# Attention and ELU feed-forward on one core: the feed-forward products and the turning of z and kv in two 128x64 column tiles

## The chip, the core and the metric

The kernel runs on one core of one Trainium2 chip. A core has a matrix engine (TensorE, PE in the profile, its weight loads listed apart as PEld), a vector engine (VectorE, DVE), a scalar engine (ScalarE, ACT), a general engine (GpSimd, POOL) and a queue engine that issues transfers (SyncE, SP). The engines run side by side and wait for each other through semaphores. The metric is the time of the kernel on the device in microseconds (us), as the median over several executions.

## What is computed

Two blocks follow each other, all in fp32. The attention block has no softmax. It makes features of queries and keys, sums over the sequence once for the whole batch, and divides:

```python
# q, k, v: (4, 4, 1088, 32); S1, S2: (8, 32)
def phi(x):                      # 64 features
    a, b = S1 x, S2 x            # 8 numbers each
    return outer(a, b)
kv  = sum over s of phi(k)[s] v[s]^T     # per batch and head, 64 x 32
z   = sum over s of phi(k)[s]            # per batch and head, 64
out = (phi(q) . kv) / (phi(q) . z + 1e-6)
```

The heads are put side by side, which gives x with 4352 tokens of 128 numbers. The second block is a feed-forward layer with 2048 hidden units:

```python
h = x @ w_in                             # 4352 x 2048
g = where(h > 0, h, exp(min(h, 0)) - 1)
return g @ w_out                         # 4352 x 128
```

The reference computes in double precision; the weights and the sketches S1, S2 arrive as 64-bit numbers and are rounded to fp32 on the core.

## The kernel before

**Tiling.** The 4352 tokens are cut into groups of 512 (the name is `g`): groups 0 to 7 have 512 tokens, group 8 has 256. The hidden units are cut into eight parts of 256 (`cp`), each of two chunks of 128 (`c`). One step of the main loop is one pair (g, cp): two products of w_in (`mm1`, into PSUM tiles `h`, one for each chunk), ELU on them (`elu`: two ScalarE instructions at L723 and L725, one VectorE instruction at L731 that writes `gg`), and two steps later the product with w_out that takes `gg` (`mm2`). The list `steps` holds the order: groups 0 and 1 alternate over cp, then groups 2 to 8 run one after the other.

**Order.** The order is written out by hand; no scheduler changes it. On each engine the instructions run in the order of the program. In step n the loop issues `mm1` of step n, then what is listed for that step under `at`, then the first ELU, what is listed under `mid`, the second ELU, what is listed under `late`, and last the w_out product of step n - 2. The attention of the later groups is listed in that way: `KF_late` (features of keys, tile `kfps`, small column and row tiles), `KA` (sums for kv and z, 32-column tiles, tile `kv`), `turn` (below), and `queries` (32x32 tiles at L493 and L589).

**Three forms of products.** A product on PE has a stationary operand, which is loaded first, and a moving one that streams through. The array can be used whole (128 rows by 128 columns) or in tiles, where a product names its tile by `tile_position`.

- Groups 0, 1 and 8 use the whole array: in `mm1` (L702), in `mm2` (L744, groups 0 and 1) and in `mm2_last` (L767, group 8). `mm1_first` (L714) is the first product of w_in.
- Groups 2 to 7 (`seven(g)`) use two tiles of 128 rows by 64 columns: `mm1` at L706 writes partitions 0 to 63 from the first 64 columns of w_in and partitions 64 to 127 from the other 64, with the same moving operand. Their second product is `mm2_seven` (L664), which computes four 64x64 blocks from seven products of sums (tiles `pa` and `pb`; the sums `tt` are made on GpSimd).
- The attention parts use smaller tiles.

**Turning.** For each batch, `Z` (L377) multiplies the sums z with a matrix of the sketch on the whole array, and `KV` (L391) turns two 128x128 blocks of kv with `nc.tensor.transpose`, also on the whole array. Batch 0 has its `Z` in `Z_first`, ahead of the main loop, followed by a filler product `keep_warm` (L218), and its `KV` in `KV_first`, step 8. Batches 1, 2 and 3 are turned by `turn` in steps 12, 20 and 28.

**Before the main loop**, the weights are rounded on VectorE and ScalarE (`RA`, `RB`, `RC`; L99 to L125), and the first tokens go through attention. PE then starts on w_out with the first L744.

The old forms are these:

```python
nc.tensor.matmul(hs[g, cp][c][:, :n], W[:, cp, c * P:c * P + P], xg[g][:, :n])            # L702
nc.tensor.matmul(hs[g, cp][c][r, :n], W[:, cp, c * P + 64 * u:c * P + 64 * u + 64],       # L706
                 xg[g][:, :n], skip_group_check=True, tile_position=(0, 64 * u))          # u = 0, 1
```

Of the kernel before, what the change touches and what calls it, by code (L numbers as in the profile page):

```python
# [27 lines left out]
def kernel(  # L28
# [21 lines left out]
    nc = tc.nc  # L50
    B, H, S, D = q.shape
    R = S1.shape[0]
    P = 128
# [92 lines left out]
    W = const.tile([P, NP, 4 * P], F32, name="W")  # L146
# [50 lines left out]
    ident = const.tile([P, P], F32, name="ident")  # L197
# [15 lines left out]

    idle = psum.tile([P, 512], F32, name="idle", tag="o0", bufs=1)

    def keep_warm(n, cols=256):
        for i in range(n):
            nc.tensor.matmul(idle[:, :cols], some[:, :P], some[:, :cols], skip_group_check=True)  # L218
# [16 lines left out]
    SXh = const.tile([P, FD], F32, name="SXh")  # L235
# [11 lines left out]
    SW = const.tile([FD, H, 3, R], F32, name="SW")  # L247
    SWq = const.tile([FD, B, 4, R], F32, name="SWq")
    keep_warm(3)
    keep_warm(1, 96)  # L250
    sps = psum.tile([P, 512], F32, name="sps", tag="aux")
    nc.tensor.matmul(sps[:, :2 * R], Sx[:].rearrange("p h d -> p (h d)"), ident[:2 * R, :2 * R])
    make_SXh()
    keep_warm(1)
    nc.vector.tensor_mul(Sab[:], _ap(sps[:, :2 * R], [[0, H], [1, 2 * R]]), _ap(bmask[:], [[1, H], [0, 2 * R]]))
    nc.gpsimd.tensor_copy(SW[:, :, :2, :].rearrange("p h x r -> p h (x r)"), Sab[:])
# [23 lines left out]
    kv_ps, kvz, feats, wzs, kf_ps = {}, {}, {}, {}, []  # L280
# [93 lines left out]

    def Z(b, ps, zl):

        nc.tensor.matmul(ps[:, 96:128], SXh[:], zl[:])  # L377

    def Z_out(b, ps):
        z = wzs[b] = SW[:, :, 2, :] if b == 0 else work.tile([FD, H, R], F32, name="wz", tag="wz")[:]  # L380
# [7 lines left out]

    def KV(b, ps):
        for f in range(2):  # L390
            nc.tensor.transpose(ps[:, 128 + P * f:128 + P * f + P], kvz[b][:, f].rearrange("p c s -> p (c s)"), ident[:])  # L391

    def KV_out(b, ps):
        nc.vector.tensor_copy(kvq[:, b].rearrange("p f h d -> p (f h d)"), ps[:, 128:384])
# [2 lines left out]
    def Z_first():  # L397
        ps = psum.tile([P, 512], F32, name="zps", tag="h", bufs=4)
        for i in range(KT):
            z_tile(0, ps, i)  # L400
        zl = ZC(0, ps)
        Z(0, ps, zl)
        Z_out(0, ps)
        keep_warm(1, 160)
# [7 lines left out]
    def KV_first():  # L412
        ps = psum.tile([P, 512], F32, name="kvps", tag="aux")
        KV(0, ps)
        KV_out(0, ps)
# [5 lines left out]
    abw, ans, qp, qpT, xg, xps = {}, {}, {}, {}, {}, {}  # L421
# [196 lines left out]
    hs, es, gs, ops = {}, {}, {}, {}  # L618
# [5 lines left out]
    def seven(g):  # L624
        return 2 <= g < NQ - 1
# [70 lines left out]
    def mm1(g, cp, cs=(0, 1)):  # L696
        n = qn[g] * P
        if 0 in cs and (g, cp) not in hs:
            hs[g, cp] = [psum.tile([P, 512], F32, name="h", tag="h", bufs=4) for c in range(2)]
        for c in cs:  # L700
            if not seven(g):
                nc.tensor.matmul(hs[g, cp][c][:, :n], W[:, cp, c * P:c * P + P], xg[g][:, :n])  # L702
                continue
            for u in range(2):
                r = slice(64 * u, 64 * u + 64)
                nc.tensor.matmul(hs[g, cp][c][r, :n], W[:, cp, c * P + 64 * u:c * P + 64 * u + 64], xg[g][:, :n],  # L706
                                 skip_group_check=True, tile_position=(0, 64 * u))

    def mm1_first():
        hs[0, 0] = [psum.tile([P, 512], F32, name="h", tag="h", bufs=4) for c in range(2)]  # L710
        for w in range(2):
            for c in range(2):
                cols = [x[:].rearrange("p (m w s) -> p w m s", w=2, s=P)[:, w] for x in (hs[0, 0][c], xg[0])]
                nc.tensor.matmul(cols[0], W[:, 0, c * P:c * P + P], cols[1], skip_group_check=True)  # L714

    def elu_a(g, cp, c, parts=(0, 1)):

# [20 lines left out]
    def mm2(g, cp, first, last):  # L738
        n = qn[g] * P
        if first:  # L740
            ops[g] = psum.tile([P, 512], F32, name="o", tag=f"o{g % 2}", bufs=1)
        gg = gs.pop((g, cp))
        for c in range(2):
            nc.tensor.matmul(ops[g][:, :n], W[:, cp, (2 + c) * P:(3 + c) * P], gg[:, c, :n],  # L744
                             start=(first and c == 0), stop=(last and c == 1))

    def fin1(g):
        n = qn[g] * P
# [11 lines left out]
    def mm2_last(cp, first, last):  # L760
        g = NQ - 1
        if first:
            ops[g] = [psum.tile([P, P], F32, name="ol", tag=t, bufs=k) for t, k in (("o0", 1), ("aux", 2))]
        gg = gs.pop((g, cp))
        for a in range(4):
            c, i = (a % 2, a // 2) if last else divmod(a, 2)
            nc.tensor.matmul(ops[g][i][:], gg[:, c, i * P:i * P + P], W[:, cp, (2 + c) * P:(3 + c) * P],  # L767
                             start=(first and c == 0), stop=(last and c == 1))

    def fin_last():  # L770
        g, n = NQ - 1, qn[NQ - 1]
# [31 lines left out]
    q5_early(0)  # L803
    q1_second()
    mm1_first()
    RA(2)
    RB(2)
    RC(1)
    elu_a(0, 0, 0)
    elu_a(0, 0, 1)  # L810
    mm1(0, 1)
    q2(1, 2)
    q4_early(1)
# [4 lines left out]
    elu_d(0, 0, 1)  # L818
    q5_early(1)
    mm2(0, 0, True, False)  # L820
    RC(3)
    for c in range(2):
# [40 lines left out]
    def turn(b):  # L863
        Z(b, kv_ps[b], zls.pop(b))
        KV(b, kv_ps[b])
# [53 lines left out]
    for n in range(2, N + 2):  # L919
        if n < N:  # L920
            g, cp = steps[n]
            mm1(g, cp)
        for f, *a in extra.get(n, ()):
            f(*a)
        if n < N:
            elu(g, cp, 0)
            if seven(g):
                sums7(g, cp, 0)
            for f, *a in extra.get((n, 0), ()):
                f(*a)  # L930
            elu(g, cp, 1)
            if seven(g):
                sums7(g, cp, 1)
        for f, *a in extra.get((n, 1), ()):
            f(*a)
        g, cp = steps[n - 2]
        if g == NQ - 1:
            mm2_last(cp, cp == 0, cp == NP - 1)
        elif seven(g):
            mm2_seven(g, cp, cp == 0, cp == NP - 1)  # L940
            if cp == NP - 1:
                fin_seven(g)
        elif n > 2:
            mm2(g, cp, cp == 0, cp == NP - 1)
            if cp == NP - 1:
                fin1(g)
# [30 lines left out]
```

## Time and profile before

| what | value |
|---|---|
| median of 5 runs | 274.61 us |
| the five runs | 272.47, 272.70, 274.61, 274.76, 275.01 us |
| profiled execution | 275.01 us, its span 273.2 us |
| granted PE clock, mean | 1.000 |
| MATMUL records: L706 / L702 / L744 / L767 | 384 / 92 / 64 / 64 |
| mean of one record: L706 / L702 / L744 | 593 / 522 / 604 ns |
| mean of one weight load: 64 columns / 128 columns | 137 / 190 ns |
| VectorE L731 (`gg`), 144 times | 652 ns each |
| ScalarE L723 and L725, 144 times each | 566 and 607 ns |
| GpSimd sums L644, L647, L648, L649, 48 times each | 754, 796, 770, 784 ns |

The profile is of one execution, the longest of the five. The records of PE overlap: a matmul's record runs from its start to the end of its results, so two that follow each other share a part, and the distance from start to start says what one costs. The weight loads run beside the products when nothing stands between. A group in the timeline ("x4") is a run of records of the same line; "128*64" is the size of the array tile in rows and columns, "128x512" the partitions and elements of the moving operand.

### The profile page before, as it was taken

The page shows a single profiled execution, that of the slowest core. Times are in us where ns is not written, and L with a number is a line of the kernel's source. Part 1 is how long each engine was busy: PE and PEld are TensorE (multiplying, and loading weights), DVE is VectorE, ACT ScalarE, POOL GpSimd, SP SyncE. Part 2 cuts the span into 40 slices and gives each one's busy share as a digit, 9 for nine tenths or more (in the row PEclk, how much of TensorE's full clock was granted, in tenths as well). Part 3 has the DMA queues.
Part 4 walks back from the last instruction along what each step waited for, and adds up shares of the span by engine and source line. Part 5 has one row for each costly group of instructions (what it writes and reads, how often), then busy time and mean ns, then how long its engine had stood idle before and what let it go on. Part 6 is the DMA issues. An engine that isn't in the chain of part 4 may idle for free.

```text
span 273.2 us, 7609 instructions
## 1 busy us (share of the span) xinstructions
PE 266.9 (98%) x3083; PEld 168.2 (62%) x3083; DVE 190.8 (70%) x350; ACT 183.5 (67%) x351; POOL 166.1 (61%) x233
## 2 busy tenths in 40 slices
PE   8999999999999999999999999999999999999994
PEld 5864444454442666666676666666766666667894
DVE  6599999996959796999548767464447444774552
ACT  2269978686564655676567667777677667777682
POOL 4500007303407986699969999988588988897200
PEclk9999999999999999999999999999999999999999
DMA  6995981001002300001100110001000200110021
GB/s 189 323 340 172 238 226 32 0 13 74 0 2 34 47 4 2 2 0 18 28 2 2 19 23 2 0 12 25 10 1 13 31 0 4 15 19 10 2 29 29
DMA packets 26419, 13.60 MB, mean 50 GB/s; under 512 B 19217, under 2 KB 24593, under 8 KB 26385
## 3 DMA queue, kind: packets, MB, share of 16 engines
q1 hardware_dynamic: 25792, 12.66, 18.8%
q8 instruction: 24, 0.39, 0.6%
q10 hardware_dynamic: 592, 0.46, 0.5%
q14 instruction: 11, 0.08, 0.1%
HBM read 10.88 MB, written 2.23 MB: 48 GB/s over the span
## 4 chain that ended last, share of the span: by engine, by line
PE 94%; DVE 4%; issue 1%; ACT 0%; DVEq 0%
PE h L706 30%; PE pb L664 16%; PE pa L664 12%; PE h L702 12%; PE o L744 11%; PE ol L767 3%; PE h L589 2%; PE idle L218 2%; PE kv L359 1%; PE abp L290 1%; PE qps L589 1%; DVE qp L536 1%; PE kfps L309 1%; PE h L493 1%; PE qps L493 1%
## 5 line engine op out<-in xcount | busy, mean ns | idle before, releaser
L731 DVE SCALAR_TENSOR_TENSOR gg<-e,h 128x512 f32<-128x512 f32 (+1 forms) x144 | 91.9, 652 | 64.7 <-ACT e L725 60.8
L723 ACT ACTIVATE e<-h 128x512 f32<-128x512 f32 (+1 forms) x144 | 81.6, 566 | 57.8 <-PE h L706 45.3
L706 PE MATMUL h<-xg,W 128*64 128x512 f32 x384 | 91.4, 593 | 0.0
L725 ACT ACTIVATE e<-e 128x512 f32<-128x512 f32 (+1 forms) x144 | 87.4, 607 | 4.6
L644 POOL TENSOR_TENSOR tt<-gg 128x256 f32<-128x256 f32 x48 | 36.2, 754 | 17.2 <-DVE gg L731 16.7
L706 PEld LDWEIGHTS h<-xg,W 128*64 128x64 f32 x384 | 27.9, 137 | 28.2 <-issue 24.9
L647 POOL TENSOR_TENSOR tt<-gg 128x256 f32<-128x256 f32 x48 | 38.2, 796 | 11.3 <-DVE gg L731 11.1
L649 POOL TENSOR_TENSOR tt<-gg,tt 128x256 f32<-128x256 f32 x48 | 37.6, 784 | 3.8
L648 POOL TENSOR_TENSOR tt<-tt,gg 128x256 f32<-128x256 f32 x48 | 37.0, 770 | 3.8
L664 PEld LDWEIGHTS pa<-gg,W 128*64 128x64 f32 x384 | 24.6, 137 | 22.4 <-issue 22.2
L702 PE MATMUL h<-xg,W 128*128 128x512 f32 (+1 forms) x92 | 36.6, 522 | 0.0
L744 PE MATMUL o<-gg,W 128*128 128x512 f32 x64 | 30.8, 604 | 0.4 <-DVE W L125 0.4
L664 PE MATMUL pa<-gg,W 128*64 128x128 f32 x384 | 30.3, 275 | 0.0
L664 PE MATMUL pb<-tt,SS 128*64 128x128 f32 x384 | 29.8, 273 | 0.0
L702 PEld LDWEIGHTS h<-xg,W 128*128 128x128 f32 x92 | 16.8, 190 | 14.9 <-issue 9.7
L664 PEld LDWEIGHTS pb<-tt,SS 128*64 128x64 f32 x384 | 23.4, 137 | 0.0
L744 PEld LDWEIGHTS o<-gg,W 128*128 128x128 f32 x64 | 11.4, 189 | 14.1 <-issue 11.9
L664 PE MATMUL pb<-gg,SS 128*64 128x128 f32 x192 | 19.5, 274 | 0.1
L664 PE MATMUL pb<-tt,W 128*64 128x128 f32 x192 | 19.4, 273 | 0.0
L122 POOL TENSOR_TENSOR raw<-raw,tiny 128x512 f32<-128x512 f32 x1 | 1.0, 1046 | 30.0 <-DVE raw L117 30.0
L664 PE MATMUL pa<-tt,SS 128*64 128x128 f32 x192 | 19.3, 273 | 0.0
L664 PEld LDWEIGHTS pb<-gg,SS 128*64 128x64 f32 x192 | 12.6, 137 | 1.0 <-issue 0.7
(141 smaller groups left out, 295.5 us busy)
## 6 DMA issues: line engine op xcount, KB each, us to landing
raw<-in_moe_w_in_dram SPq DMA_DIRECT2D x8, 256.0 KB, 5.8
raw<-in_moe_w_out_dram SPq DMA_DIRECT2D x8, 256.0 KB, 5.9
hd_k<-in_k_dram SPq DMA_DIRECT2D x3, 544.0 KB, 8.3
hd_q<-in_q_dram SPq DMA_DIRECT2D x3, 544.0 KB, 3.6
v<-in_v_dram SPq DMA_DIRECT2D x4, 288.0 KB, 6.8
out_dram<-ob SPq DMA_DIRECT2D x72, 16.0 KB, 1.5
v<-in_v_dram SPq DMA_DIRECT2D x4, 256.0 KB, 8.4
out_dram<-ob SPq DMA_DIRECT2D x16, 32.0 KB, 1.7
```

Of the source, the lines that this page charges most:

```text
L589: nc.tensor.matmul(ps[c][D * h:D * h + D, 64 * k:64 * (k + m)], kvq[r, b, f, h, :], qpT[g, i][r, n * o + 2 * k:n * o + 2 * (k + m), f, :], ...
L644: nc.gpsimd.tensor_tensor(t[:, 0], b12, b11, op=SUB)
L647: nc.gpsimd.tensor_tensor(t[:, 2], b22, b12, op=SUB)
L648: nc.gpsimd.tensor_tensor(t[:, 1], t[:, 2], b11, op=ADD)
L649: nc.gpsimd.tensor_tensor(t[:, 3], b21, t[:, 1], op=SUB)
L664: nc.tensor.matmul(bank[64 * u:64 * u + 64, P * col:P * col + P], lhs, rhs[:, u], start=(first and i in (0, 3)), stop=last, skip_group_che ...
L702: nc.tensor.matmul(hs[g, cp][c][:, :n], W[:, cp, c * P:c * P + P], xg[g][:, :n])
L706: nc.tensor.matmul(hs[g, cp][c][r, :n], W[:, cp, c * P + 64 * u:c * P + 64 * u + 64], xg[g][:, :n], skip_group_check=True, tile_position=( ...
L723: nc.scalar.activation(e, hs[g, cp][c][:, :n], RELU, scale=-1.0)
L725: nc.scalar.activation(e, e, EXP, scale=-1.0)
L731: nc.vector.scalar_tensor_tensor(gs[g, cp][:, c, :n], es[g, cp][:, c, :n], -1.0, hs[g, cp][c][:, :n], op0=ADD, op1=MAX)
L744: nc.tensor.matmul(ops[g][:, :n], W[:, cp, (2 + c) * P:(3 + c) * P], gg[:, c, :n], start=(first and c == 0), stop=(last and c == 1))
```

## The change

A helper `halves` issues one product as two, in the two 128x64 column tiles. It takes the place of every whole-array product from the first one of w_in on: `mm1_first`, `mm1` (where it also takes the place of the loop that groups 2 to 7 had), `mm2` and `mm2_last`; and of `Z` for all four batches and of the transposes in `KV`, which become products with the identity as moving operand. The filler products, the transposes of query features in `q4_early` and the transpose in `KS_first` stay on the whole array. Nothing else is changed, and the order of the program is the same.

```diff
+    def halves(dst, lhs, rhs, **kw):
+        for u in range(2):
+            nc.tensor.matmul(dst[64 * u:64 * u + 64], lhs[:, 64 * u:64 * u + 64], rhs, skip_group_check=True,
+                             tile_position=(0, 64 * u), **kw)
...
     def Z(b, ps, zl):
 
-        nc.tensor.matmul(ps[:, 96:128], SXh[:], zl[:])
+        halves(ps[:, 96:128], SXh[:], zl[:])
...
     def KV(b, ps):
         for f in range(2):
-            nc.tensor.transpose(ps[:, 128 + P * f:128 + P * f + P], kvz[b][:, f].rearrange("p c s -> p (c s)"), ident[:])
+            halves(ps[:, 128 + P * f:128 + P * f + P], kvz[b][:, f].rearrange("p c s -> p (c s)"), ident[:])
...
         for c in cs:
-            if not seven(g):
-                nc.tensor.matmul(hs[g, cp][c][:, :n], W[:, cp, c * P:c * P + P], xg[g][:, :n])
-                continue
-            for u in range(2):
-                r = slice(64 * u, 64 * u + 64)
-                nc.tensor.matmul(hs[g, cp][c][r, :n], W[:, cp, c * P + 64 * u:c * P + 64 * u + 64], xg[g][:, :n],
-                                 skip_group_check=True, tile_position=(0, 64 * u))
+            halves(hs[g, cp][c][:, :n], W[:, cp, c * P:c * P + P], xg[g][:, :n])
...
-                nc.tensor.matmul(cols[0], W[:, 0, c * P:c * P + P], cols[1], skip_group_check=True)
+                halves(cols[0], W[:, 0, c * P:c * P + P], cols[1])
...
         for c in range(2):
-            nc.tensor.matmul(ops[g][:, :n], W[:, cp, (2 + c) * P:(3 + c) * P], gg[:, c, :n],
-                             start=(first and c == 0), stop=(last and c == 1))
+            halves(ops[g][:, :n], W[:, cp, (2 + c) * P:(3 + c) * P], gg[:, c, :n],
+                   start=(first and c == 0), stop=(last and c == 1))
...
-            nc.tensor.matmul(ops[g][i][:], gg[:, c, i * P:i * P + P], W[:, cp, (2 + c) * P:(3 + c) * P],
-                             start=(first and c == 0), stop=(last and c == 1))
+            halves(ops[g][i][:], gg[:, c, i * P:i * P + P], W[:, cp, (2 + c) * P:(3 + c) * P],
+                   start=(first and c == 0), stop=(last and c == 1))
```

## The prediction

> **What bounds the kernel now.** I read the page first, then the chain of waits, then the timeline of TensorE (PE) at each place where the form of its products changes, then the waits and the busy times by stretches.
>
> From the page:
>
> ```profile
> span 273.2 us, 7609 instructions
> ...
> PE 266.9 (98%) x3083; PEld 168.2 (62%) x3083; DVE 190.8 (70%) x350; ACT 183.5 (67%) x351; POOL 166.1 (61%) x233
> ...
> PE 94%; DVE 4%; issue 1%; ACT 0%; DVEq 0%
> ```
>
> PE is busy for 98% of the span and is 94% of the chain. So what counts is not whether PE works but how densely its products follow each other. From the chain of waits (start, length, line):
>
> ```profile
> 33.34 1.72 PE o L744 x4
> 35.05 1.72 PE h L702 x4
> ...
> 90.53 0.87 PE pb L664 x16
> ...
> 153.44 1.72 PE h L706 x8
> ...
> 258.18 0.89 PE ol L767 x8
> 259.07 0.87 PE h L702 x4
> ```
>
> An fp32 product shows as two MATMUL records (L744: 32 products, 64 records), two passes. Two full 128x512 products (x4) take 1.72 us, 430 ns a pass. The same two products as 64-column halves (L706, x8) take 1.72 us too: the halves of a pass run side by side. So splitting a long product gains nothing by itself. At 128 columns there is a small difference: eight half-tile passes (pb, x16) take 0.87 us, 109 ns each, eight full ones (ol, x8) 0.89 us, 112 ns.
>
> The loss is at the seams. The timeline of PE in the stretch where products of w_in are already halves and those of w_out not yet:
>
> ```profile
> 81.45 1.98 PE L744 MATMUL o<-gg,W 128*128 128x512 f32 x4
> 83.36 1.94 PE L706 MATMUL h<-xg,W 128*64 128x512 f32 x8
> 85.23 1.98 PE L744 MATMUL o<-gg,W 128*128 128x512 f32 x4
> 87.14 1.94 PE L706 MATMUL h<-xg,W 128*64 128x512 f32 x8
> 89.01 0.72 PE L309 MATMUL kfps<-kT,Sxp 64*32 64x288 f32 x16
> ```
>
> From start to start a full group takes 1.91 us here and a half-tile group 1.87, where 1.72 is what the passes need. So each change of form costs a full group about 0.20 us and a half-tile group 0.15. In the records of the passes 0.095 of it is the gap before the first weight load of the new form. The rest is that load, in the open: 0.107 us for 128 columns, 0.053 for 64. The same at the end, where group 8 (full) meets group 7 (halves):
>
> ```profile
> 251.56 1.13 PE L702 MATMUL h<-xg,W 128*128 128x256 f32 x4
> 252.63 0.66 PE L664 MATMUL pa<-gg,W 128*64 128x128 f32 x8
> ...
> 254.31 1.13 PE L702 MATMUL h<-xg,W 128*128 128x256 f32 x4
> ```
>
> 251.56 to 252.63 is 1.07 us for what takes 0.87 among its own kind (259.07 above), again 0.20. The half-tile group takes 1.68 for 14 passes of 109 ns (1.53), again 0.15.
>
> **The change part by part.** The order of the instructions on all engines stays. PE gets 260 more MATMUL records: 236 by splitting (L702 92, L714 8, L744 64, L767 64, L377 8) and 24 because eight transposes of one record become sixteen half products of two. No DMA is added, taken or moved, so no queue is passed.
>
> 1. *Splitting long products, inside a run of one form:* 0. The cover is the other half; without it each pass would take twice as long, so the two rows of 1.72 above are the whole argument.
>
> Here a rule speaks against the change. The trace's row: in the half-tile products the second half starts 7 ns after the first and the next pass follows after 429 ns, as for full ones. The Trainium skill, "TensorEngine Tiling (Array Packing)", section Instruction Overhead, gives each matmul about 60 cycles of overhead, and its section When to Use Tiling keeps column tiles for stationary operands of at most 64 columns. At the 2.4 GHz of "TensorE: Matmul & The Clock Gate" (section on the HAM clock gate) 60 cycles are 25 ns; over the 236 added records that is, as an estimate from these pages, 5.9 us, and the kernel would end at about 274.6 + 5.9 - 2.1 = 278.4 us. By the row it is 0. I take the row: it is 384 records of this very form in this kernel.
>
> 2. *Entries into full products from small tiles* (after key features, kv sums and queries: 40.78, 59.70, 67.95, 77.02, 81.45) and the first w_out product at 24.49, which opens with a load after waiting for W: the load in the open becomes 0.053 instead of 0.107. The gap itself stays. 6 x 0.053 = -0.32 us.
>
> 3. *The stretch 78 to 89:* three changes full to half (0.095 + 0.053) and one half to full (0.095 + 0.107) go: -0.44 - 0.20 = -0.65 us.
>
> 4. *The end:* three half to full and two full to half: -0.61 - 0.30 = -0.90 us.
>
> 5. *Last w_out products (L767):* 64 passes at 109 instead of 112 ns: -0.18 us.
>
> 6. *Turning z and kv.* The transposes now, and a turn among half-tile groups:
>
> ```profile
> 47.75 0.38 PE L391 MATMUL kvps<-ident,kvl 128*128 128x128 f32 x2
> 47.97 1.02 PE L744 MATMUL o<-gg,W 128*128 128x512 f32 x2
> ```
>
> ```profile
> 97.79 0.41 PE L377 MATMUL kv<-zl,SXh 128*128 128x32 f32 x2
> 98.03 0.42 PE L391 MATMUL kv<-ident,kvl 128*128 128x128 f32 x2
> 98.38 0.66 PE L664 MATMUL pa<-gg,W 128*64 128x128 f32 x8
> ```
>
> Two transposes take 0.22 us, one pass each. As products with the identity they need two passes of 109 ns: 0.44. Batch 0: +0.22. Batch 1 (63.24 to 63.64, 0.40 now) needs 0.44 plus two 32-column passes for z; a pass of that size, half-tile, is 55 to 58 ns in L456. That makes 0.55: +0.15. Batches 2 and 3 cost 0.095 + 0.59 + 0.053 = 0.74 now, with a change of form on both sides, and 0.55 then: -0.19 each. Sum -0.01 us. Here the trace has no identity product; bounds are +0.1 and +0.8 against the transposes alone (the load hidden or 53 ns open at each half), and I take the pa row.
>
> 7. *Before 24.49 us:* 0. The half-tile z of batch 0 is ready some 0.07 us sooner, but the filler product after it now changes form twice, and the next products start within 0.03 us of where they do now. The first w_in products lose one change of form and the query transposes behind them gain one (+-0.20). That lies under the rounding of W on VectorE (DVE), which is what PE waits for at 24.49:
>
> ```profile
> PE o L744 <- DVE W L125: 0.4, 1, 0.4
> ```
>
> It is also PE's last wait of this kind in the view of waits. If that cover were gone the first part could cost or bring 0.2.
>
> Added waits: some two dozen of L731 get a wait on PE beside the one on ScalarE. The product they wait for is read by ScalarE first, so it is past; where L731 has this wait already it is a 21 ns entry beneath the running instruction.
>
> Sum: -0.32 - 0.65 - 0.90 - 0.18 - 0.01 = -2.06 us. The profiled execution took 275.01 (span 273.2 and 1.8 around it): 272.95 by it. It is the longest of the five; against their median 274.61 the sum gives 272.55.
>
> **Rivals.** *A: another engine takes the place of PE where PE gets faster.* DVE is nearly full in one stretch:
>
> ```profile
> 40.00:60.00 20.00, 20.00 (x150) 9.44 (x150) 19.73 (x30) 15.79 (x27) 7.25 (x4) 1.00 0.11 26
> ```
>
> But in that stretch the change makes PE no faster (items 2 and 6: -0.1, +0.22). Where it gains, margins are small but there: the output of group 1 is turned on DVE until 89.19, and pb, in the same bank, is first written at 90.5, to come 0.7 sooner; near 260.5 the products of step (8,4) wait for DVE to free h at 260.18 and 260.51, 0.4 to 0.6 ahead of use, with 0.26 gained since DVE's chain began. GpSimd's last sums are done at 254.85 and used at 256.7. Were items 3 and half of 4 eaten up, 1.1 us would be lost again: 273.5.
>
> *B, slower: PE's instruction stream.* The change adds some 520 entries to PE's 6166 (260 loads, 260 products), half of them between 18 and 90 us, where PE's count per 20 us now is as low as 65 matmuls; instructions come by DMA, and the engines' DMA share is 0.92 and 0.76 in the first two stretches of 20 us. A block arriving late would stop PE for about what a transfer takes there, 5.8 us from issue to landing for a piece of w_in. One such stop: 274.61 - 2.06 + 5.8 = 278.3; it decides from 2.1 us of stop on. Against it: PE shows no stop of this kind now, also not where it runs 228 matmuls in the first 20 us.
>
> *C: the change does not do what it says:* the halves do not overlap for the identity or for gg as stationary operand. For gg and W with 128 columns pa speaks against it. If only the turning ran one half after the other, 4 x 0.44 = +1.8 us: 274.3.
>
> **Numbers.** Forecast case 0.72; A 0.13; C 0.05; B or another loss of over 2 us 0.10. The runs before spread over 2.5 us (272.47 to 275.01), so the median of the changed kernel may lie 1 us either way of 272.6 in the likeliest case: 271.2 to 273.8. The range takes in A, and the lower end of the runs before less the sum (272.47 - 2.06 = 270.4): 270.4 to 274.5. About 1% is what a measurement can tell from no change; faster by more means below 271.9. The sum is 0.75%, so that needs a third more than it: 0.27. Within 1%: 0.65. Slower by over 1%: 0.08.
>
> **What would show it.** In the trace after: 3343 matmul records; every start-to-start of two long products 1.72 us between 78.9 and 89 and 0.87 for the 256-column pairs after 249; last products 2.62 instead of 2.69 us for the final 24 passes; a turn of 0.55 us without gaps around it; PE's first wait still for W at 24.5. Wrong would be: passes over 435 ns in the split groups, PE waiting for DVE or GpSimd after 77 us, or turns over 0.8 us.

## The result and the profile after

The changed kernel has a median of 272.49 us (38 runs, 270.46 to 273.54) beside 274.43 us for the kernel before on the same chips (75 runs, 272.37 to 275.77). The medians differ by 1.94 us. The ratio is 0.9932, with a 95% interval from 0.9917 to 0.9947: a gain of 0.7%, within the 1% that the prediction named as "no change". The profiled execution took 272.02 us.

The page of the kernel after:

```profile
span 270.2 us, 8153 instructions
...
PE 264.0 (98%) x3343; PEld 160.7 (59%) x3343; DVE 191.2 (71%) x350; ACT 183.4 (68%) x351; POOL 165.8 (61%) x233
...
PE 94%; DVE 4%; issue 1%; ACT 0%; DVEq 0%
```

PE has the 3343 records that were forecast, is still 98% busy and still 94% of the chain. The other engines do what they did. So the kernel is bound by the same engine, whose work became a little denser. From the chain of waits (start, length, line):

```profile
47.03 0.44 PE kvps L219 x8
...
255.42 0.87 PE ol L219 x16
256.29 0.86 PE h L219 x8
...
264.10 2.64 PE ol L219 x48
```

The last products take 0.87 and 2.64 us instead of 0.89 and 2.69. The turning of batch 0 takes 0.44 us. The timeline of PE at the places that the prediction showed of before (start, length, line, output<-inputs, array tile, moving operand, count):

```profile
46.86 0.61 PE L219 MATMUL kvps<-ident,kvl 128*64 128x128 f32 x8
47.30 1.03 PE L219 MATMUL o<-gg,W 128*64 128x512 f32 x4
...
80.49 1.94 PE L219 MATMUL o<-gg,W 128*64 128x512 f32 x8
82.26 1.89 PE L219 MATMUL h<-xg,W 128*64 128x512 f32 x8
83.98 1.89 PE L219 MATMUL o<-gg,W 128*64 128x512 f32 x8
85.69 1.89 PE L219 MATMUL h<-xg,W 128*64 128x512 f32 x8
...
96.19 0.26 PE L219 MATMUL kv<-zl,SXh 128*64 128x32 f32 x4
96.27 0.64 PE L219 MATMUL kv<-ident,kvl 128*64 128x128 f32 x8
96.74 0.61 PE L670 MATMUL pa<-gg,W 128*64 128x128 f32 x8
...
249.60 1.03 PE L219 MATMUL h<-xg,W 128*64 128x256 f32 x8
250.47 0.61 PE L670 MATMUL pa<-gg,W 128*64 128x128 f32 x8
...
251.99 1.03 PE L219 MATMUL h<-xg,W 128*64 128x256 f32 x8
```

Read the starts, not the lengths. 82.26 to 83.98 to 85.69 is 1.72 and 1.71 us, where the same groups took 1.87 and 1.91 before. The first group, 80.49 to 82.26, still takes 1.77 (1.91 before): it comes after small tiles, so the form still changes there, and a load of about 0.05 us stays in the open. A turn among its own form, 96.19 to 96.74, takes 0.55 us instead of 0.74 with its two seams. At the end, 249.60 to 250.47 is 0.87 instead of 1.07, and the 14 passes of the next group take 1.52 instead of 1.68.

PE's first wait for the rounding of W is what it was, and after it no wait for VectorE or GpSimd has taken the place of the seams. From the view of PE's waits (times in us: total, number, longest):

```profile
PE o L219 <- DVE W L125: 0.4, 1, 0.4
```

**The ledger.** Both traces were cut at the same products and the pieces subtracted, start to start. The stretch from the start of the first w_out product (24.49 in before) to the start of the last matmul record, called *main stretch* below, is 244.88 us long in before and 242.75 in after. It is 2.12 us shorter; the forecast was 2.06.

| step of the prediction | forecast, us | measured, us |
|---|---|---|
| 2 and 3: entries, stretch 78 to 89 | -0.97 | -0.94 |
| 4: the end | -0.90 | -0.89 |
| 5: last w_out products | -0.18 | -0.15 |
| 6: turning, batches 0, 1, then 2 and 3 together | +0.22, +0.15, -0.38 | +0.22, +0.16, -0.37 |
| not in the sum: a shorter wait in step 15 | 0 | -0.155 |
| sum | -2.06 | -2.12 |

Each measured row is good to about 0.01 us, as small rests were laid to one piece or the next.

The spans of the two profiled executions differ by more, 2.99 us: 0.73 lies ahead of the first changed instruction, in the first 10 us (last section), 0.06 between the first sums for z and the first w_out product, where a kernel that leaves this part as before shows the same 0.05, and 0.08 behind the last product.

### The profile page after: what moved, and what is told of

Same layout as the page of the kernel before. It is cut to its first block, busy times and chain, and to the rows that moved or that the text cites. A ratio compares the mean times of both kernels' runs of the same rounds, so it can differ in the third digit from the quotient of the medians.

```text
span 270.2 us, 8153 instructions
## 1 busy us (share of the span) xinstructions
PE 264.0 (98%) x3343; PEld 160.7 (59%) x3343; DVE 191.2 (71%) x350; ACT 183.4 (68%) x351; POOL 165.8 (61%) x233
## 4 chain that ended last, share of the span: by engine, by line
PE 94%; DVE 4%; issue 1%; ACT 0%; DVEq 0%
PE h L219 42%; PE pb L670 16%; PE pa L670 12%; PE o L219 11%; PE ol L219 3%; PE idle L224 2%; PE h L595 2%; PE kv L365 1%; PE abp L296 1%; PE qps L595 1%; DVE qp L542 1%; PE kfps L315 1%; PE h L499 1%; PE qps L499 1%; PE kv L219 1%
## 5 line engine op out<-in xcount | busy, mean ns | idle before, releaser
L219 PE MATMUL h<-xg,W 128*64 128x512 f32 (+1 forms) x584 | 129.4, 563 | 0.0
L219 PEld LDWEIGHTS h<-xg,W 128*64 128x64 f32 x584 | 42.2, 137 | 46.0 <-issue 37.1
L219 PE MATMUL o<-gg,W 128*64 128x512 f32 x128 | 30.5, 597 | 0.4 <-DVE W L125 0.4
L219 PEld LDWEIGHTS o<-gg,W 128*64 128x64 f32 x128 | 8.5, 136 | 16.0 <-issue 13.6
L670 PEld LDWEIGHTS pb<-tt,W 128*64 128x64 f32 x192 | 12.8, 137 | 0.3 <-POOL tt L655 0.3
L670 PEld LDWEIGHTS pa<-tt,SS 128*64 128x64 f32 x192 | 12.8, 137 | 0.0
```

What stands on the lines that cost most here:

```text
L219: nc.tensor.matmul(dst[64 * u:64 * u + 64], lhs[:, 64 * u:64 * u + 64], rhs, skip_group_check=True, tile_position=(0, 64 * u), **kw)
L670: nc.tensor.matmul(bank[64 * u:64 * u + 64, P * col:P * col + P], lhs, rhs[:, u], start=(first and i in (0, 3)), stop=last, skip_group_che ...
```

## The experiments

Theory: the gain is made of changes of form that are gone, each worth 0.15 to 0.20 us, and splitting itself costs nothing. Rivals: the gain lies in one part only; part of it comes from somewhere else, such as a wait; or the split has a price of its own, covered here by something larger. Every kernel below ran beside the kernel before on the same chip.

**1. The end alone.** The kernel before, with halves for group 8 only.

```diff
+            if g == NQ - 1:
+                halves(hs[g, cp][c][:, :n], W[:, cp, c * P:c * P + P], xg[g][:, :n])
+                continue
...
-            nc.tensor.matmul(ops[g][i][:], gg[:, c, i * P:i * P + P], W[:, cp, (2 + c) * P:(3 + c) * P],
+            halves(ops[g][i][:], gg[:, c, i * P:i * P + P], W[:, cp, (2 + c) * P:(3 + c) * P],
```

> The kernel before, with only the products of group 8 (its two w_in products a step and its w_out products) in two 64-column tiles. Theory (seams: 0.20 us for each entry into the whole array, 0.15 us for each return): the five changes of form after 249 us go (-0.90) and 64 passes take 109 instead of 112 ns (-0.18): 273.4 us, 1.08 under the kernel before, all of it after the first w_in product of group 8; the stretch before that unchanged. Rival A (another engine binds at the end): less than half of it, 0.5 us or less. Rival B (longer instruction stream): no gain or a loss.

Median 273.12 beside 274.67 us, ratio 0.9949 (0.9926 to 0.9971). The main stretch is 1.04 us shorter than before: 0.90 from turn 3 to the first `ol` product and 0.15 in the last products. The pieces ahead of group 8 are what they were, to 0.02 us. Rival A would have left 0.5 us or less, rival B no gain. Steps 4 and 5 hold by themselves.

**2. Groups 0 and 1 alone.** The kernel before, with halves in `mm1_first`, in `mm1` for the first two groups and in `mm2`.

```diff
+            if g < 2:
+                halves(hs[g, cp][c][:, :n], W[:, cp, c * P:c * P + P], xg[g][:, :n])
+                continue
...
-            nc.tensor.matmul(ops[g][:, :n], W[:, cp, (2 + c) * P:(3 + c) * P], gg[:, c, :n],
+            halves(ops[g][:, :n], W[:, cp, (2 + c) * P:(3 + c) * P], gg[:, c, :n],
```

> The kernel before, with only the w_in and w_out products of groups 0 and 1 in two 64-column tiles; turning and group 8 stay on the whole array. Theory: entries from small tiles and the stretch 78 to 89 bring -0.32 and -0.65, but the turns of batches 0 and 1 now stand between half-tile products and pay both seams, 0.35 us each: +0.70. Together -0.3 us, and in the trace one seam pair around each of the first two turns. Rival (the gain comes from the shorter weight loads of the split products, not from seams): most of 2 us already here, since 78 of the 110 split feed-forward products are in these groups.

Median 273.74 beside 274.67 us, ratio 0.997 (0.9952 to 0.9988); the main stretch is 0.59 us shorter, twice what was expected. The stretch from the key features at 80.8 to those at 89.0 us gives 0.545, as it does in the changed kernel, and the two turns, now alone in their form, pay for their seams nearly as expected (+0.30 and +0.34 in place, where 0.35 each was expected). What was not expected is 0.3 us at the queries of step 15. The timeline of PE and VectorE there, first in before, then after, then in this kernel:

```profile
73.20 1.88 PE L702 MATMUL h<-xg,W 128*128 128x512 f32 x4
75.02 0.61 PE L589 MATMUL h<-qpT,kvq 32*32 32x64 f32 x5
...
75.39 0.31 PE L589 MATMUL h<-qpT,kvq 32*32 32x64 f32 x2
...
77.02 0.70 PE L744 MATMUL o<-gg,W 128*128 128x512 f32 x1
...
74.57 0.65 DVE L731 SCALAR_TENSOR_TENSOR gg<-e,h 128x512 f32<-128x512 f32 x1
```

```profile
72.60 1.89 PE L219 MATMUL h<-xg,W 128*64 128x512 f32 x8
74.41 0.48 PE L595 MATMUL h<-qpT,kvq 32*32 32x64 f32 x5
...
74.62 0.31 PE L595 MATMUL h<-qpT,kvq 32*32 32x64 f32 x2
...
76.26 1.94 PE L219 MATMUL o<-gg,W 128*64 128x512 f32 x8
...
73.89 0.65 DVE L731 SCALAR_TENSOR_TENSOR gg<-e,h 128x512 f32<-128x512 f32 x1
```

```profile
73.43 1.89 PE L219 MATMUL h<-xg,W 128*64 128x512 f32 x8
75.24 0.31 PE L595 MATMUL h<-qpT,kvq 32*32 32x64 f32 x2
...
75.28 0.30 PE L595 MATMUL h<-qpT,kvq 32*32 32x64 f32 x2
...
76.93 1.94 PE L219 MATMUL o<-gg,W 128*64 128x512 f32 x8
...
74.52 0.65 DVE L740 SCALAR_TENSOR_TENSOR gg<-e,h 128x512 f32<-128x512 f32 x1
```

The queries write into a tile `h` that VectorE's `gg` still reads. In before the first query products start at 75.02 and the next row of `h` follows only 0.37 us later; `gg` ends at 74.57 + 0.65 = 75.22. After, PE comes at 74.41 and `gg` ends at 74.54: the pause is shorter, 0.21. In this kernel PE is held up by the seams of turn 1, comes at 75.24, `gg` has ended at 75.17, and there is no pause. The whole block of queries takes 2.00, 1.85 and 1.69 us. So this wait can take up a loss of time ahead of it: it is shorter than before by 0.155 us in the changed kernel and by 0.31 here. That most of the 2 us is won in groups 0 and 1 is ruled out.

**3. Turning as before.** The changed kernel, with `Z` and `KV` whole again.

```diff
-        halves(ps[:, 96:128], SXh[:], zl[:])
+        nc.tensor.matmul(ps[:, 96:128], SXh[:], zl[:])
...
-            halves(ps[:, 128 + P * f:128 + P * f + P], kvz[b][:, f].rearrange("p c s -> p (c s)"), ident[:])
+            nc.tensor.transpose(ps[:, 128 + P * f:128 + P * f + P], kvz[b][:, f].rearrange("p c s -> p (c s)"), ident[:])
```

> The changed kernel, with z and kv turned on the whole array as before (transposes of one pass). Theory: every turn now pays two seams (0.35 us) and saves passes (0.22 us, batches 1 to 3 about 0.16 net of z): batch 0 +0.13, batches 1 to 3 +0.19 each, 0.70 us over the changed kernel, 273.2 us. Rival (the identity products are the more costly part, as two passes for one): faster than the changed kernel by up to 0.9 us (four turns, 0.22 each).

Median 272.22 us (11 runs), ratio 0.9923 (0.9895 to 0.9951): in the medians not to be told from the changed kernel. The trace tells more. The main stretch is 0.49 us longer than in the changed kernel: 0.65 in place (+0.08, then +0.19 for each of batches 1 to 3), of which the queries of step 15, late again and so without a pause, give back 0.16. Turn 2 in the timeline of PE:

```profile
93.13 1.89 PE L219 MATMUL h<-xg,W 128*64 128x512 f32 x8
94.94 0.41 PE L383 MATMUL kv<-zl,SXh 128*128 128x32 f32 x2
95.19 0.42 PE L397 MATMUL kv<-ident,kvl 128*128 128x128 f32 x2
95.53 0.66 PE L670 MATMUL pa<-gg,W 128*64 128x128 f32 x8
```

94.94 to 95.53 is 0.59 us, and the group ahead takes 1.81 instead of 1.72: two changes of form. A transpose has half the passes, yet among half tiles the identity product is the cheaper form (0.55 us for the turn). This kernel is experiments 1 and 2 put together, and the parts add: 1.04 + 0.59 + 0.49 = 2.12 us, the whole gain.

**4. A change of form where there was none.** The changed kernel, with `mm2` of groups 0 and 1 whole: full and half-tile groups alternate through 16 steps.

```diff
-            halves(ops[g][:, :n], W[:, cp, (2 + c) * P:(3 + c) * P], gg[:, c, :n],
+            nc.tensor.matmul(ops[g][:, :n], W[:, cp, (2 + c) * P:(3 + c) * P], gg[:, c, :n],
```

> The changed kernel, with the w_out products of groups 0 and 1 on the whole array, so that the form changes twice in every step up to 90 us. Theory: 16 returns to half tiles at 0.148, 10 entries from half tiles at 0.202, 6 entries from small tiles or a wait at 0.053 more: 4.7 us over the changed kernel, 277.2 us. Rival (the stretch up to 77 us is bound by VectorE, busy for 19.7 of 20 us, so that PE has slack there): only the part after 77 us shows, 0.7 us, 273.2 us.

Median 277.4 beside 274.67 us, ratio 1.0109 (1.0076 to 1.0141). The main stretch is 4.67 us longer than in the changed kernel. The timeline of PE:

```profile
51.27 1.94 PE L219 MATMUL h<-xg,W 128*64 128x512 f32 x8
53.14 1.98 PE L744 MATMUL o<-gg,W 128*128 128x512 f32 x4
55.05 1.94 PE L219 MATMUL h<-xg,W 128*64 128x512 f32 x8
56.92 1.98 PE L744 MATMUL o<-gg,W 128*128 128x512 f32 x4
```

1.87 and 1.91 us from start to start, the figures of the seams in before, now at every step. Nothing hides them: that VectorE sets the pace until 77 us is ruled out.

**5. Four tiles instead of two.** The changed kernel, with every pair of halves, and the products of `mm2_seven`, as four 128x32 tiles.

```diff
-        for u in range(2):
-            nc.tensor.matmul(dst[64 * u:64 * u + 64], lhs[:, 64 * u:64 * u + 64], rhs, skip_group_check=True,
-                             tile_position=(0, 64 * u), **kw)
+        for u in range(4):
+            nc.tensor.matmul(dst[32 * u:32 * u + 32], lhs[:, 32 * u:32 * u + 32], rhs, skip_group_check=True,
+                             tile_position=(0, 32 * u), **kw)
...
```

> The changed kernel, with every product that it splits in two (and the seven products of groups 2 to 7) split in four 128x32 column tiles. This doubles the matmul records of the feed-forward part, some 2,700 more, and gives it the form that the sums for kv and z have. Theory (tiles of one pass run side by side, only changes of form cost): the two seams around the sums of batches 1 to 3 go (about 0.25 us each), the load in the open at 11 other entries falls from 0.053 to about 0.027 (-0.3), against some 13 ns more lag of the last tile at each seam: about 0.8 us under the changed kernel, 271.7 us, if four loads of 32 columns still fit into a pass of 109 ns. Rival ([...] an instruction stream that comes too late): far slower, [...] idle PE without a semaphore for the second.

Median 272.97 beside 274.48 us, ratio 0.9951 (0.9929 to 0.9974). The trace has 5575 records, 2232 more than the changed kernel. A steady step of groups 2 to 7 takes 3.245 us with four tiles as with two, so splitting is free here too. The seams around the 32-column kv sums are gone as expected (-0.10 us ahead of the kv sums of batch 1, -0.23 behind them, -0.19 between turns 2 and 3, against the changed kernel). But the main stretch is 0.28 us longer, not 0.8 shorter. About 0.45 is small losses in the later steps; 0.55 is one stop. The timeline of PE (the bracket gives idle time and what ended it):

```profile
93.60 0.42 PE L670 MATMUL pb<-tt,W 128*32 128x128 f32 x3
94.39 0.31 PE L670 MATMUL pb<-tt,W 128*32 128x128 f32 x3 [0.38 <-issue]
```

In the middle of one product's passes PE stands, and no semaphore ends it: the profile puts it down to issue. It is the kind of stop that rival B feared, but of 0.55 us where that put 5.8.

**6. Four tiles up to step 30, then two.** As 5, with the number of tiles a variable that is set to 2 after `mm1` of step 30.

```diff
...
+        if n == 30:
+            cut[0] = 2
```

> Four 128x32 tiles up to the w_in product of step 30, two 128x64 tiles from there on; the switch lies at the queries of step 30, where the form changes anyway. Theory: the seams around the sums of batches 1 to 3 go as they did with four tiles throughout (0.33, 0.35 and 0.19 us in the stretches that hold them), and the small losses of the later steps with four tiles do not come: 0.6 to 0.8 us from the first w_out product to the last matmul under the changed kernel, 242.0 us instead of 242.75, if the stop of 0.55 us at 94 us was a chance of that run; 242.6 if the stop is part of this instruction stream. Rival (denser instructions always cost as much as the seams they save): 243.0, like four tiles throughout.

Median 272.39 beside 274.32 us, ratio 0.992 (0.9892 to 0.9948). The small losses of the later steps are gone: from turn 3 to the first `ol` product it takes 128.49 us, as the changed kernel does. The stop is there again, 0.94 us, at the same product (91.89 to 93.08 us in its trace). The main stretch is 242.91 us, 241.97 without the stop.

**7. Number 5 once more.** No edit.

> Four 128x32 tiles throughout, once more. If the stop of 0.55 us of PE at 94 us, without a semaphore, belongs to the instruction stream, it is there again at the same product (last product into pb of that step); if it was a chance of one run, it is gone and the stretch from the first w_out product to the last matmul is 242.5 instead of 243.0 us.

271.59 us in its one execution. The view of PE's waits and the timeline:

```profile
PE pb L670 <- issue: 1.0, 1, 1.0
```

```profile
92.34 0.41 PE L670 MATMUL pb<-tt,W 128*32 128x128 f32 x3
93.73 0.31 PE L670 MATMUL pb<-tt,W 128*32 128x128 f32 x3 [0.97 <-issue]
```

The stop returns at the same product, now 1.14 us. In all three traces it comes after PE's 2753rd record (weight loads and products counted together), and PE goes on 1.33 to 1.45 us after the end of a 16 KB transfer on the instruction queue. The later that transfer ended, 0.68, 0.40 and 0.18 us ahead of the last pass before the stop, the longer the stop: 0.55, 0.94 and 1.14 us. It belongs to the program, not to one execution; its length varies. The small losses of the later steps vary too: 0.30 us here, 0.45 in experiment 5.

**8. The changed kernel once more.** No edit.

> The changed kernel once more, beside the two others on the same chip. From the first w_out product to the last matmul 242.75 us again, within 0.1; the time before that may differ by up to 2 us, as it did between the runs so far.

272.47 us (18 runs), ratio 0.9933 (0.9911 to 0.9956); the main stretch is 242.74 us, as at first, and its steps agree to 0.01 us. Its trace has no such stop. So with two tiles, differences of 0.05 us between pieces of two traces can be read; the two traces with four tiles throughout differ by more.

**9. Four tiles only where they save a seam:** up to step 15, and from step 22 to 30.

```diff
...
+        if n in (15, 22, 30):
+            cut[0] = 6 - cut[0]
```

> The changed kernel, with four 128x32 tiles only up to the queries of step 15 and from the queries of step 22 to those of step 30, that is around the sums of batches 1 and 3 but not of batch 2, where PE stopped. Theory (the stop is late instructions: it always came after PE's 2753rd instruction, and fewer instructions before it spare it): no stop, 0.35 to 0.4 us saved around batch 1 and 0.2 around batch 3, so 242.2 us from the first w_out product to the last matmul, 0.55 under the changed kernel, some 271.9 us as the median. Rival (the stop goes with the place in the program, not with the count of instructions): a stop of 0.5 to 1.1 us again near 93 us, 243 us or more. Second rival: another place stops instead, since the blocks end elsewhere.

Median 271.89 us (6 runs) beside 274.65, ratio 0.9889 (0.9856 to 0.9921). With 3907 records there is no stop. The main stretch is 242.61 us, of which 0.40 is a delay at 33 us, where PE waits for ScalarE in an execution whose first queries came late. The view of PE's waits:

```profile
PE abqp L453 <- DVE qT L241: 1.9, 1, 1.9
...
PE o L222 <- ACT kvl L377: 0.2, 1, 0.2
```

Without the 0.40 it would be 242.2, as expected; that the late queries caused it is not shown. The pieces with fewer seams are shorter than in the changed kernel: 10.74 instead of 10.84 us from the turn of batch 0 to the sums of batch 1, 4.60 instead of 4.83 from there to the turn, and 30.24 instead of 30.57 between turns 2 and 3. So this form would be 0.5 us faster than the changed kernel, 0.15 of which the trace shows as it stands. In the medians its interval overlaps that of the changed kernel, so the lead is not settled. The absence of the stop does not tell the count of instructions from the place: in this kernel the steps around 93 us have two tiles again.

## Why the prediction was right

**Steps 1 to 3.** Splitting costs nothing: the split groups keep 1.72 us, and experiment 5 splits them once more for nothing. Here the trace's row gave the forecast, and not the rule of the Trainium skill that was weighed against it ("TensorEngine Tiling (Array Packing)", section Instruction Overhead): 2232 more matmul records left the steady step at 3.245 us. The entries and the stretch brought 0.94 of the 0.97 us forecast.

**Steps 4 and 5** brought 0.89 and 0.15 (forecast 0.90 and 0.18), in experiment 1 the same without the rest of the change.

**Step 6** came out batch by batch. Its sum of -0.01 must not be read as "leave it alone": it is counted from before. Once the neighbours are half tiles, whole turns would cost 0.49 us (experiment 3).

**Step 7** holds: 0.06 us, which is also there without any change in that part.

**What was overlooked** is one term: the wait of the queries of step 15 for VectorE's `gg`. The view of waits lists it only in a sum over four places, and the prediction had it neither as a cost nor as a reserve. It changed by 0.155 us in favour, because PE reaches the place with less lead over VectorE. The prediction had no reason for this gain: that it about makes up for what other steps fell short is luck. Such a wait also returns part of a loss ahead of it, so that a loss measured in place (0.65 in experiment 3) is more than the end sees (0.49).

**Rival A** has no row in the trace: VectorE and GpSimd delay PE nowhere that they did not before. (Two figures of its passage are a little off: `pb` is first written at 90.36 us, not at 90.5, and 1.1 us lost again would make some 273.7, not 273.5. Neither bears on the outcome.) **Rival B** did not occur here, but its mechanism seems to exist: with four tiles PE stops by 0.55 to 1.14 us without a semaphore. That instructions arrive late is inferred (the same place in the program, no semaphore, a nearly fixed time behind a transfer on the instruction queue, gone with fewer instructions there) and not shown; why just there, and how near the changed kernel is to it, stays open. **Rival C** is excluded by a turn of 0.44 us in batch 0 and of 0.55 in batch 2.

The sum, taken from the profiled execution, gave 272.95 us; that execution of the new kernel took 272.02. Of the difference 0.73 is the first 10 us, which the change does not touch, and the rest small (the wait of step 15, step 5, the two ends). The median, 272.49, lies so near the other forecast, 272.55, in part by luck: the starts alone move an execution by more than that (last section).

## What to carry to other kernels

Where one engine is nearly always busy, measure from start to start in the timeline: the price of a seam shows only there, not in busy shares. A product is then best given the form of its neighbours, even if that doubles its passes, as long as the added passes (0.22 us for two transposes here) cost less than the two seams they save (0.30 to 0.34 as measured in experiment 2). Add up such small savings by place, and ask of each wait behind them whether it will give some of it back.

## What the hardware showed unexpectedly

**A change of form has a price of its own.** In alternation (experiment 4) each change costs 0.15 or 0.20 us, of which 0.095 is a gap; the rest is a weight load that otherwise runs beside the products.

**PE's speed in the first 10 us differs between executions of equal code.** The same products, ahead of every change, by the view of one tile (duration min/median/max in ns, first and last start) in before, after and experiment 3:

```profile
L444 PE MATMUL abqp<-Sab,qT x16: 314/314/368, 9.0 to 10.1; 128*64 128x64 f32 x16
```

```profile
L450 PE MATMUL abqp<-Sab,qT x16: 222/222/270, 8.9 to 9.5; 128*64 128x64 f32 x16
```

```profile
L450 PE MATMUL abqp<-Sab,qT x16: 222/222/270, 7.6 to 8.1; 128*64 128x64 f32 x16
```

One takes 314 ns in before and 222 in the others; the first sums for z start at 10.38, 9.65 and 8.26 us. The row of the granted clock shows full speed in all three. The Trainium skill, "TensorE: Matmul & The Clock Gate", in its section on the HAM clock gate, has PE start at a lower clock and rise after a time of work that varies from run to run; the durations fit that, but no row here shows a lower clock.

The start shows in the time: the two profiled executions of the changed kernel (the first one and experiment 8) took 272.02 and 272.51 us, 0.49 apart. Their first sums for z start 0.50 us apart (9.65 and 10.14), and their main stretches agree to 0.01 us.

The times of both kernels bunch at two levels some 2 us apart (most of before at 274.1 to 275.1 and a good part at 272.4 to 273.1; the changed kernel at 272.1 to 273.5 and 270.5 to 271.4). A spread of 2.1 us at the start is enough for that; that it is the cause of the bunches is not shown. The spread is as large as the whole effect of this change. It is a likely reason why experiment 3 looks no slower in its median: five of its 11 runs lie in the lower bunch, but only ten of the changed kernel's 38. Within the bunches its medians are higher, 271.06 beside 270.88 us and 273.13 beside 272.56, though with few runs.
